# The first six heads' queries by chunks of the model dimension, the general path on one queue, and the row sums counted on VectorE

## The chip, the cores and the metric

The kernel runs on one core of a Trainium2 chip. The metric is device time in microseconds (us), the median of several runs. The engines that matter here are TensorE (PE in the profile; its weight loads are PEld), VectorE (DVE), ScalarE (ACT), GpSimd (POOL) and SyncE (SP), which here only issues transfers and waits. A "q" behind an engine's name (SPq, ACTq) means its instruction sequencer.

## What is computed

Two problems, A and B, of the same shape: queries from an activation `x`, attention over a cache of keys and values with grouped heads (32 query heads, 4 key heads), and an output projection. B = 16 sequences, 32 queries each (512 tokens), model dimension 1024, 512 keys, head size 128, all bfloat16.

```python
q = (x @ wq).reshape(B, Sq, Hq, Dh).transpose(0, 2, 1, 3)
k = jnp.repeat(k_cache, rep, axis=1)          # rep = 8
v = jnp.repeat(v_cache, rep, axis=1)
p = softmax(einsum("bhqd,bhkd->bhqk", q, k) * Dh ** -0.5)
o = einsum("bhqk,bhkd->bhqd", p, v)
out = o.transpose(0, 2, 1, 3).reshape(B, Sq, Hq * Dh) @ wo
# the result is the concatenation of A's and B's out along the last axis
```

## The kernel before

The kernel has two paths. `fast_path` computes everything with a constant shift in the exponential in place of the row's maximum. It keeps the reciprocals of all softmax sums in `rall`, and at the end counts how many of them lie between two limits. If all do, its result stands; if not, `general_path` computes everything anew with the row maximum. With the inputs here the count is full, so the general path is built into the program but not executed: each engine loads the count `ok_i` into a register (L642), compares it and jumps to a short block for the branch not taken (L644), in which the semaphores that the general path would have moved are waited for and brought forward. Then all engines meet at the closing barriers (L671).

The fast path's instructions stand in the order in which they are written (`manual_schedule`), engine by engine.

The beginning: `x` of A (512 tokens by 1024) is loaded in four pieces of 128 whole rows (`load_x`, L469), with the first weights between them. `wq_tiles[0, 0]` and `wq_tiles[0, 1]` hold 4 heads each. `warm_up` runs matmuls on zeros. `transpose_x(tt)` turns one piece of 128 rows into all eight 128-row chunks of `xT` (L507, copies at L510). `first_heads` (L517) computes heads 0 and 1 for the first 256 tokens, and after the other two pieces for the rest. Then `run(units, 52)` issues heads 2 to 7 and 4 matmuls of head 8 from a stream of units. A unit is one matmul of 512 columns: 8 make up a head's queries (`q_units`, L312, copied out by ScalarE at L320), 32 make up a tile of the output projection (`f_units`, L331, copied at L340, stored at L342).

The main loop has 128 slots, one for each pair of a sequence and a key head. A slot issues the loads that a plan gives it, the scores (L368) with their exponential (L376), the values (L432) of four slots before, and 6 or 7 units from the stream in between. Column sums go over VectorE and a small matmul (L387, L396, L404, L413). Loads of K (transposed by the transfer), V, `wq` and `wo` all go through SyncE's queue; stores of the output go through GpSimd's, but for the last two tiles, of 256 columns, which SyncE and ScalarE store.

The end: two passes over `rall` on VectorE (L626) count the flags for each of 32 partitions, 16 units are issued, a matmul with a column of ones adds the partitions (`ok_ps`, L634), VectorE copies the count out (L635), and the remaining units follow. The registers are loaded after all of it.

Of the kernel before, what the change touches and what calls it, by code (L numbers as in the profile page):

```python
# [16 lines left out]
P = 128  # L17
HQ = 32
# [12 lines left out]
def general_path(tc, problems, out_flat):  # L31
# [11 lines left out]
    with ExitStack() as ctx:  # L43
# [10 lines left out]
        for x, k_cache, v_cache, wq, wo, col_off in problems:  # L54
            x_v = x.flatten_outer_dims().rearrange("(t p) d -> p t d", p=P)
            x_sb = wpool.tile([P, TT, D], BF16, name="g_x", tag="g_w")
            nc.sync.dma_start(out=x_sb[:], in_=x_v)
# [10 lines left out]
            for c in range(HQ // WH):  # L68
                wq_sb = wpool.tile([P, DC, WH * DH], BF16, name="g_wq", tag="g_w")
                nc.sync.dma_start(  # L70
                    out=wq_sb[:], in_=wq_v[:, :, c * WH * DH:(c + 1) * WH * DH]
                )
                for hl in range(WH):
                    q_ps = psum.tile([P, NTOK], FP32, name="g_q_ps", tag="g_p", bufs=2)
                    for dc in range(DC):
                        nc.tensor.matmul(
                            q_ps[:],
                            lhsT=wq_sb[:, dc, hl * DH:(hl + 1) * DH],
                            rhs=xT[:, dc, :],
                            start=(dc == 0),  # L80
                            stop=(dc == DC - 1),
                        )
                    nc.scalar.mul(
                        out=qT[:, :, c * WH + hl, :],
                        in_=q_ps[:].rearrange("p (b s) -> p b s", s=SQ),
                        mul=SCALE,
                    )
            oT = big.tile([P, HQ, NTOK], BF16, name="g_oT")
            k_rows = k_cache.rearrange("b g k d -> (b g k) d")
            for b in range(B):  # L90
                kT = kvpool.tile([P, HKV, SK], BF16, name="g_kT")
                r0 = b * HKV * SK
                nc.sync.dma_start_transpose(out=kT[:], in_=k_rows[r0:r0 + HKV * SK, :])
                v_sb = kvpool.tile([P, HKV, KC, DH], BF16, name="g_v")
                nc.sync.dma_start(
                    out=v_sb[:], in_=v_cache[b].rearrange("g (c p) d -> p g c d", p=P)
                )
                for g in range(HKV):
# [53 lines left out]
            for oc in range(NOUT // OCW):  # L152
                wo_sb = wpool.tile([P, HQ, OCW], BF16, name="g_wo", tag="g_w")
                nc.sync.dma_start(out=wo_sb[:], in_=wo_v[:, :, oc * OCW:(oc + 1) * OCW])
                for tt in range(TT):
                    f_ps = psum.tile([P, OCW], FP32, name="g_f_ps", tag="g_p", bufs=2)
                    for h in range(HQ):
                        nc.tensor.matmul(
                            f_ps[:],
                            lhsT=oT[:, h, tt * P:(tt + 1) * P],  # L160
                            rhs=wo_sb[:, h, :],
                            start=(h == 0),
                            stop=(h == HQ - 1),
                        )
                    o_sb = work.tile([P, OCW], BF16, name="g_o_sb")
                    nc.vector.tensor_copy(out=o_sb[:], in_=f_ps[:])
                    c0 = col_off + oc * OCW
                    nc.sync.dma_start(
                        out=out_flat[tt * P:(tt + 1) * P, c0:c0 + OCW], in_=o_sb[:]
                    )  # L170
# [3 lines left out]
def kernel(  # L174
# [35 lines left out]
    def fast_path(ok_i):  # L210
        with ExitStack() as fctx:
# [9 lines left out]
            tc.mark_branch_hint_location(  # L221
                "general",
                "LikelyTaken",
                [nc.sync.engine, nc.scalar.engine, nc.vector.engine, nc.tensor.engine, nc.gpsimd.engine],
            )
# [3 lines left out]
            warm = work.tile([P, NW], BF16, name="warm", tag="p_sb", bufs=6)  # L229
# [10 lines left out]
            one_col = const.tile([P, 1], FP32, name="one_col")  # L240
            nc.vector.memset(one_col[:], 1.0)
            shift = const.tile([P, 1], FP32, name="shift")
            nc.vector.memset(shift[:], SHIFT)
            cnt = const.tile([P, 1], FP32, name="cnt")
            nc.vector.memset(cnt[:], 0.0)
# [35 lines left out]
            def load_k(j):  # L281
                ks = kv_part(j, 1)
                kT = k_tiles[j] = kv.tile([P, GRP, SK], BF16, name="kT")
                if j < NG // GRP:
                    for q in range(GRP):
                        nc.sync.dma_start_transpose(out=kT[:, q, :], in_=ks[q])
# [178 lines left out]
            wq_tiles[0, 0] = blk_tile([P, DC, 4 * DH], "wq_sb")  # L465
            HC = DC // 2

            def load_x(tt):
                nc.sync.dma_start(out=x_sb[:, tt, :], in_=x_v[:, tt, :])  # L469

            def load_first_wq(ns, cs):
                nc.sync.dma_start(out=wq_tiles[0, 0][:, cs, ns], in_=wq_v[:, cs, ns])  # L472

            load_x(0)
            load_x(1)
            load_first_wq(slice(0, 2 * DH), slice(0, HC))
            load_first_wq(slice(0, 2 * DH), slice(HC, DC))
            load_x(2)
            load_x(3)
            load_first_wq(slice(2 * DH, 4 * DH), slice(0, DC))  # L480
            load_wq(0, 1)
            load_k(0)
            load_v(0)
            load_wq(0, 2)
# [3 lines left out]
            warm_ps = psum.tile([P, NW], FP32, name="warm_ps", tag="sums", bufs=1)  # L488

            def warm_up(n):  # L490
                for _ in range(n):
                    nc.tensor.matmul(  # L492
                        warm_ps[:], lhsT=warm[:, 0:P], rhs=warm[:], start=True, stop=True
                    )
# [3 lines left out]
            def transpose_x(tt):  # L498
                ts = slice(tt * P, (tt + 1) * P)
                bank = ("ob", "proj", "sums", "ob")[tt]  # L500
                for cs, where_, copy in (
                    (slice(0, HC), dict(tag="s"), nc.vector.tensor_copy),
                    (slice(HC, DC), dict(tag=bank, bufs=2 if bank == "proj" else 1), nc.scalar.copy),
                ):
                    xT_ps = psum.tile([P, HC, P], BF16, name="xT_ps", **where_)
                    for k, dc in enumerate(range(cs.start, cs.stop)):
                        nc.tensor.transpose(  # L507
                            xT_ps[:, k, :], x_sb[:, tt, dc * P:(dc + 1) * P], ident[:]
                        )
                    copy(out=xT[0][:, cs, ts], in_=xT_ps[:])  # L510

            qT[0, 0] = blk_tile([P, B, REP, SQ], "qT")

            def first_heads(h, t0, t1, dcs):
                ts = slice(t0 * P, t1 * P)
                for dc in dcs:
                    nc.tensor.matmul(  # L517
                        first_q[h][:, ts],
                        lhsT=wq_tiles[0, 0][:, dc, h * DH:(h + 1) * DH],
                        rhs=xT[0][:, dc, ts],  # L520
                        start=(dc == 0),
                        stop=(dc == DC - 1),
                    )

            lower, upper = range(HC), range(HC, DC)
            warm_up(5)
            transpose_x(0)
            transpose_x(1)
            first_q = [psum.tile([P, NW], FP32, name="q_ps", tag="proj") for _ in range(2)]
            warm_up(2)  # L530
            for dcs in (lower, upper):
                for h in range(2):
                    first_heads(h, 0, 2, dcs)
            transpose_x(2)
            transpose_x(3)
            for h in range(2):
                for tt in (2, 3):
                    first_heads(h, tt, tt + 1, range(DC))
            for h, copy in enumerate((nc.vector.tensor_copy, nc.scalar.copy)):
                copy(  # L540
                    out=qT[0, 0][:, :, h, :],
                    in_=first_q[h][:].rearrange("p (b s) -> p b s", s=SQ),
                )

            def stream():
                for h in range(2, HQ):
# [6 lines left out]
                for tts in ((0, 1), (2,)):  # L553
                    for nh in range(NH):
                        for tt in tts:
                            yield from f_units(1, tt, nh * NW, NW, nc.gpsimd)
# [5 lines left out]
            run(units, (REP - 2) * DC + 4)  # L562
# [59 lines left out]
            sq = blk_tile([QD, NG * 2 * REP], "sq", FP32)  # L622
            cnt2 = const.tile([P, 2], FP32, name="cnt2")
            nc.vector.memset(cnt2[:], 0.0)
            for k, (lim, op) in enumerate(((1.0 / SUM_HI, ALU.is_ge), (1.0 / SUM_LO, ALU.is_le))):
                nc.vector.tensor_scalar(  # L626
                    out=sq[:], in0=rall[0:QD].rearrange("p j n -> p (j n)"),
                    scalar1=lim, scalar2=0.0, op0=op, op1=ALU.add,
                    accum_out=cnt2[0:QD, k:k + 1],
                )  # L630
            nc.vector.tensor_tensor(out=cnt[:], in0=cnt2[:, 0:1], in1=cnt2[:, 1:2], op=ALU.add)
            run(units, 16)
            ok_ps = psum.tile([1, 1], FP32, name="ok_ps", tag="s")
            nc.tensor.matmul(ok_ps[:], lhsT=cnt[:], rhs=one_col[:], start=True, stop=True)  # L634
            nc.vector.tensor_copy(out=ok_i[:], in_=ok_ps[:])  # L635
            run(units, 1 << 20)

    flag = ctx.enter_context(tc.tile_pool(name="flag", bufs=1))
    ok_i = flag.tile([1, 1], I32, name="ok_i")
    fast_path(ok_i)  # L640
    total = 2 * 2 * NG * QW
    ok = nc.values_load(ok_i[0:1, 0:1], min_val=0, max_val=total,  # L642
                        skip_runtime_bounds_check_because="only compared")
# [32 lines left out]
```

## Time and profile before

| | |
|---|---|
| median of 6 runs | 348.68 us (347.97 to 348.80) |
| profiled execution | 348.74 us |
| its span, first to last instruction | 346.8 us |
| TensorE busy | 338.7 us, 2145 matmuls |
| VectorE, ScalarE busy | 265.8 and 189.2 us |
| bytes moved by transfers | 71.70 MB, 207 GB/s over the span |
| `L331` (output projection), 512-column matmuls | 127.6 us busy |
| `L312` (queries), 512-column matmuls | 124.1 us busy |
| last matmul ends | 342.46 us |

The span is shorter than the time of its execution by what lies before the first and behind the last instruction. Matmuls overlap in the pipeline, so the profile's mean duration of one (366 ns at L331) is longer than the distance between two starts; that distance is read from a row of many matmuls. A row of the timeline has the start, the time from the first instruction's start to the last one's end, the engine, the line, the operation, the tile written and the tiles read, the shape and the number of instructions; in brackets how long the engine had been idle before and what ended that. A row of one line's instructions has the engine, the operation and its number, the shortest, median and longest duration in ns, and the start of the first and the last.

### The profile page before, as it was taken

The numbers are of one execution on the slowest core, as the hardware profiler recorded it, in microseconds if no ns is written. First come the engines' busy times: TensorE is split into PE (matmuls) and PEld (weight loads), VectorE is DVE, ScalarE is ACT, GpSimd is POOL, SyncE is SP. The second block draws the span as 40 slices with busy tenths as digits, with TensorE's granted clock in tenths as the row PEclk, the third lists the DMA queues.
The fourth block names the chain that finished last, engine by engine and source line by source line (L and its number), as shares of the span: only waits on it lengthen the run. The fifth ranks groups of instructions, "written<-read, shape, count | busy, mean of one in ns | idle before, by whom it ended". The sixth has DMA issues, their size and how long they took to land.

```text
span 346.8 us, 5422 instructions
## 1 busy us (share of the span) xinstructions
PE 338.7 (98%) x2145; PEld 218.2 (63%) x2185; DVE 265.8 (77%) x340; ACT 189.2 (55%) x213; POOL 8.9 (3%) x21
## 2 busy tenths in 40 slices
PE   8999999999999999999999999999999999999994
PEld 5556666666666666666666666666666666666554
DVE  2117888888888888888888888888988888888610
ACT  2447666666666766666655445555455545555000
POOL 0000000000000000000000000000000000000010
PEclk9999999999999999999999999999999999999999
DMA  7999999999998999999999449995669984400000
GB/s 227 240 306 339 166 256 263 263 262 260 274 203 191 217 243 237 291 271 272 271 307 205 109 127 289 350 255 122 137 188 290 295 210 115 114 33 2 15 33 19
DMA packets 125068, 71.70 MB, mean 207 GB/s; under 512 B 73616, under 2 KB 124048, under 8 KB 125040
## 3 DMA queue, kind: packets, MB, share of 16 engines
q1 hardware_dynamic: 124176, 69.29, 81.4%
q0 software_dynamic: 720, 1.97, 1.6%
q8 instruction: 18, 0.29, 0.4%
q14 instruction: 10, 0.08, 0.1%
q10 hardware_dynamic: 144, 0.07, 0.1%
HBM read 51.38 MB, written 2.10 MB: 154 GB/s over the span
## 4 chain that ended last, share of the span: by engine, by line
PE 96%; DMA 2%; issue 1%; SPq 1%; ACT 0%; ACTq 0%
PE f_ps L331 31%; PE q_ps L312 30%; PE ob L432 17%; PE s_ps L368 17%; DMA x_sb<-in_A_x_dram 2%; PE q_ps L517 1%; SPq L469 0%; SPq L472 0%; PE xT_ps L507 0%; PE sums L404 0%; ACT o_sb L340 0%; PE ok_ps L634 0%; SPq L671 0%; ACTq L340 0%
## 5 line engine op out<-in xcount | busy, mean ns | idle before, releaser
L376 ACT ACTIVATE p_sb<-s_ps,shift 128x1024 bf16<-128x1024 f32 x128 | 142.7, 1115 | 101.6 <-PE s_ps L368 69.4
L387 DVE TRANSPOSE_TENSOR_REDUCE parts<-p_sb 128x32 f32<-128x1024 bf16 x128 | 158.9, 1241 | 45.6 <-ACT p_sb L376 45.5
L331 PE MATMUL f_ps<-wo_sb,oT 128*128 128x512 bf16 (+1 forms) x524 | 127.6, 366 | 0.5
L312 PE MATMUL q_ps<-xT,wq_sb 128*128 128x512 bf16 x476 | 124.1, 379 | 0.5
L432 PE MATMUL ob<-p_sb,v_sb 128*128 128x256 bf16 x512 | 76.8, 273 | 0.7
L368 PE MATMUL s_ps<-qT,kT 128*128 128x256 bf16 x512 | 76.8, 273 | 0.5
L331 PEld LDWEIGHTS <-oT 128*128 128x128 bf16 x544 | 53.0, 98 | 34.8
L368 PEld LDWEIGHTS <-kT 128*128 128x128 bf16 x512 | 56.9, 113 | 24.7
L312 PEld LDWEIGHTS <-wq_sb 128*128 128x128 bf16 x496 | 48.5, 98 | 35.8 <-DMA wq_sb<-in_A_wq_dram 0.2
L432 PEld LDWEIGHTS <-v_sb 128*128 128x128 bf16 x512 | 50.1, 98 | 19.9
L454 DVE TENSOR_TENSOR oT<-r,ob 128x512 bf16<-128x512 f32 x64 | 44.0, 687 | 8.8 <-PE ob L432 2.3
L320 ACT CAST qT<-q_ps 128x512 bf16<-128x512 f32 x62 | 36.2, 584 | 21.1 <-PE q_ps L312 19.0
L418 DVE STREAM_TRANSPOSE r<-rall 128x512 f32<-128x512 f32 x64 | 44.2, 691 | 1.1
L340 ACT CAST o_sb<-f_ps 128x512 bf16<-128x512 f32 (+1 forms) x17 | 9.5, 559 | 23.2 <-PE f_ps L331 14.6
L342 POOL DMA_DIRECT2D out_dram<-o_sb x15 | 8.2, 550 | 327.3 <-ACT o_sb L340 327.3
L396 DVE TENSOR_REDUCE cs<-parts 128x32 fp32r<-128x128 f32 x32 | 12.0, 375 | 1.1
L404 PE MATMUL sums<-cs,fold 128*128 128x32 f32 x32 | 11.7, 367 | 0.0
L413 DVE RECIPROCAL rall<-sums 128x32 f32<-128x32 f32 x32 | 10.2, 320 | 0.5 <-PE sums L404 0.5
L404 PEld LDWEIGHTS sums<-cs,fold 128*128 128x128 f32 x32 | 6.1, 190 | 3.8
L510 DVE COPY xT<-xT_ps 128x512 bf16<-128x512 bf16 x4 | 1.7, 424 | 5.5 <-PE xT_ps L507 5.5
L510 ACT COPY xT<-xT_ps 128x512 bf16<-128x512 bf16 x4 | 2.3, 586 | 5.6 <-PE xT_ps L507 5.5
L492 PE MATMUL warm_ps<-warm 128*128 128x512 bf16 x7 | 3.2, 597 | 1.3 <-DVE warm L230 1.3
(26 smaller groups left out, 21.9 us busy)
## 6 DMA issues: line engine op xcount, KB each, us to landing
v_sb<-in_A_v_cache_dram SPq DMA_DIRECT2D x16, 512.0 KB, 4.3
wq_sb<-in_B_wq_dram SPq DMA_DIRECT2D x8, 1024.0 KB, 6.2
wo_sb<-in_A_wo_dram SPq DMA_DIRECT2D x8, 1024.0 KB, 6.7
v_sb<-in_B_v_cache_dram SPq DMA_DIRECT2D x16, 512.0 KB, 4.3
wo_sb<-in_B_wo_dram SPq DMA_DIRECT2D x8, 1024.0 KB, 8.9
wq_sb<-in_A_wq_dram SPq DMA_DIRECT2D x7, 1024.0 KB, 7.3
out_dram<-o_sb POOLq DMA_DIRECT2D x15, 128.0 KB, 2.1
x_sb<-in_A_x_dram SPq DMA_DIRECT2D x4, 256.0 KB, 4.1
```

The lines of the kernel that those rows point to most:

```text
L312: nc.tensor.matmul(ps[:], lhsT=w[:, dc, (h % 4) * DH:(h % 4 + 1) * DH], rhs=xT[pr][:, dc, :], start=(dc == 0), stop=(dc == DC - 1),)
L320: nc.scalar.copy(out=qT[pr, g][:, :, hl, :], in_=ps[:].rearrange("p (b s) -> p b s", s=SQ),)
L331: nc.tensor.matmul(ps[:, 0:width], lhsT=oT[pr, tt][:, h, :], rhs=wo_tiles[pr, nh, h // REP][:, h % REP, off:off + width], start=(h == 0), ...
L368: nc.tensor.matmul(s_ps[:, c, :], lhsT=kT[:, i % GRP, c, :], rhs=qT[pr, g][:, b, :, :].rearrange("p h s -> p (h s)"), start=True, stop=True,)
L376: nc.scalar.activation(out=p_sb[:], in_=s_ps[:], func=ACTF.Exp, bias=shift[:], scale=SCALE)
L387: nc.vector.tensor_reduce(out=parts[k][:, q, :, :].rearrange("p c h -> p (c h)"), in_=st[i]["p"][:].rearrange("p c (h s) -> p (c h) s", s=SQ),
L396: nc.vector.tensor_reduce(out=cs[:], in_=parts.pop(k)[:].rearrange("p q c h -> p q h c"), axis=AX.X, op=ALU.add,)
L404: nc.tensor.matmul(sums[:], lhsT=fold[:].rearrange("p r s -> p (r s)"), rhs=cs[:].rearrange("p q h -> p (q h)"), start=True, stop=True,)
L413: nc.vector.reciprocal(out=rall[:, k, :], in_=quad.pop(k)[:])
L418: nc.vector.transpose(out=r[:].rearrange("p n s -> p (n s)"), in_=rall[:, k, o * 2 * REP:(o + 1) * 2 * REP] .unsqueeze(2).to_broadcast([P, ...
L432: nc.tensor.matmul(ob[j][:, q, :], lhsT=v_sb[:, i % GRP, c, :], rhs=st[i]["p"][:, c, :], start=(c == 0), stop=(c == KC - 1),)
L454: nc.vector.tensor_tensor(out=out, in0=rcp.pop(j)[:].rearrange("p (q h) s -> p q h s", h=REP), in1=ob.pop(j)[:].rearrange("p q (h s) -> p ...
```

## The change

- The beginning goes by chunks of the model dimension. `x` is loaded in four column pairs of two 128-column chunks each (the first pair in two halves of 256 tokens), in runs of 512 bytes. The weights of heads 0 to 7 lie in two tiles `w0`, each with four 128-row chunks of all eight heads, loaded after the piece of `x` that they meet. `transpose_x(k)` transposes chunks 2k and 2k+1 for all tokens. Six PSUM accumulators, heads 0 to 5, take one chunk after the other; the transposes of the next pair stand in the middle of every second chunk. Heads 6 and 7 follow with all eight chunks each. The copies are shared between VectorE and ScalarE. The warm-ups are 128 columns wide: 19 before the transposes, 2 and 4 between them.
- The order of the first loads: one quarter of the first K block, then `wq` for heads 8 to 11, then the rest of K, and V. Before: two blocks of `wq` with all of the first K and V between them.
- 5 units of head 8 are issued before the main loop; it was 4.
- The stores of B's first two token tiles go through SyncE's queue instead of GpSimd's.
- The count: the flags' sums are added by a 32x32 block transpose and a reduction on VectorE; the matmul is gone. The registers are loaded 40 units after it, in the middle of TensorE's last stretch, and not at the end.
- In the general path every transfer is issued by GpSimd; K is loaded as it lies and transposed on TensorE.
- The mark for the branch hint stands near the end of the fast path in the text.

```diff
 # general_path, at each of its transfers
-            nc.sync.dma_start(out=x_sb[:], in_=x_v)
+            nc.gpsimd.dma_start(out=x_sb[:], in_=x_v)
...
-                nc.sync.dma_start_transpose(out=kT[:], in_=k_rows[r0:r0 + HKV * SK, :])
+                for g in range(HKV):
+                    kT_ps = psum.tile([P, KC, P], BF16, name="g_kT_ps", tag="g_t", bufs=2)
+                    for kc in range(KC):
+                        nc.tensor.transpose(kT_ps[:, kc, :], k_sb[:, g, kc, :], ident[:])
...
 # fast_path, the beginning
-            load_x(0)
-            load_x(1)
-            load_first_wq(slice(0, 2 * DH), slice(0, HC))
-            load_first_wq(slice(0, 2 * DH), slice(HC, DC))
-            load_x(2)
-            load_x(3)
-            load_first_wq(slice(2 * DH, 4 * DH), slice(0, DC))
-            load_wq(0, 1)
-            load_k(0)
-            load_v(0)
-            load_wq(0, 2)
+            w0 = [blk_tile([P, HC, REP * DH], "w0_sb") for _ in range(2)]
+            def load_x(k, ts=slice(0, TT)):
+                cs = slice(2 * k * P, (2 * k + 2) * P)
+                nc.sync.dma_start(out=x_sb[:, ts, cs], in_=x_v[:, ts, cs])
+            load_x(0, slice(0, TT // 2))
+            load_x(0, slice(TT // 2, TT))
+            load_w0(slice(0, 1), slice(0, HALF * DH))
+            load_w0(slice(0, 1), slice(HALF * DH, REP * DH))
+            load_w0(slice(1, 2))
+            for k in range(1, DC // 2):
+                load_x(k)
+                load_w0(slice(2 * k, 2 * k + 2))
+            load_k(0, slice(0, 1))
+            load_wq(0, 2)
+            load_k(0, slice(1, GRP))
+            load_v(0)
             load_k(1)
             load_v(1)
...
-            warm_up(5)
-            transpose_x(0)
-            transpose_x(1)
-            ...
+            warm_up(19)
+            transpose_x(0, (2, 4))
+            ...
+            for dc in range(DC - 2):
+                for h in range(NF):
+                    if dc % 2 and h == NF // 2:
+                        transpose_x(dc // 2 + 1)
+                    first_head(first_q[h], h, dc)
+            for h in (0, 2, 4, 1, 3, 5):
+                for dc in (DC - 2, DC - 1):
+                    first_head(first_q[h], h, dc)
+                evacuate(first_q[h], h)
+            for h, tag in zip(range(NF, REP), ("ob", "sums")):
+                q_ps = psum.tile([P, NW], FP32, name="q_ps", tag=tag, bufs=1)
+                for dc in range(DC):
+                    first_head(q_ps[:], h, dc)
+                evacuate(q_ps[:], h)
...
-                for tts in ((0, 1), (2,)):
+                for tts, eng in (((0, 1), nc.sync), ((2,), nc.gpsimd)):
...
-            run(units, (REP - 2) * DC + 4)
+            run(units, 5)
 # the end
-            nc.vector.tensor_tensor(out=cnt[:], in0=cnt2[:, 0:1], in1=cnt2[:, 1:2], op=ALU.add)
-            run(units, 16)
-            ok_ps = psum.tile([1, 1], FP32, name="ok_ps", tag="s")
-            nc.tensor.matmul(ok_ps[:], lhsT=cnt[:], rhs=one_col[:], start=True, stop=True)
-            nc.vector.tensor_copy(out=ok_i[:], in_=ok_ps[:])
-            run(units, 1 << 20)
+            nc.vector.transpose(out=tally_t, in_=tally)
+            nc.vector.tensor_reduce(out=cnt, in_=tally_t[0:1], axis=AX.X, op=ALU.add)
+            nc.vector.tensor_copy(out=ok_i[:], in_=cnt)
+            run(units, 40)
+            tc.mark_branch_hint_location(...)
+            ok = nc.values_load(ok_i[0:1, 0:1], min_val=0, max_val=total, ...)
+            run(units, 1 << 20)
+            return ok
```

## Prediction

> **What bounds the kernel now.** I first read the page's busy shares and its chain of waits, to see which engine sets the end.
>
> ```profile
> PE 338.7 (98%) x2145; PEld 218.2 (63%) x2185; DVE 265.8 (77%) x340; ACT 189.2 (55%) x213; POOL 8.9 (3%) x21
> ...
> PE 96%; DMA 2%; issue 1%; SPq 1%; ACT 0%; ACTq 0%
> ```
>
> Columns of the first: busy time, share, instructions; the second is the chain's shares. TensorE carries 96% of it; only the stretch before its steady stream and the one after its last matmul are left. So I read the timeline of the first 12 us next.
>
> ```profile
> 1.29 2.31 PE L492 MATMUL warm_ps<-warm 128*128 128x512 bf16 x5 [1.29 <-DVE warm L230]
> ...
> 3.63 1.89 PE L507 MATMUL xT_ps<-ident,x_sb 128*128 128x128 bf16 x16
> ...
> 4.28 0.42 DVE L510 COPY xT<-xT_ps 128x512 bf16<-128x512 bf16 x1 [1.82 <-PE xT_ps L507]
> ...
> 5.31 0.84 PE L492 MATMUL warm_ps<-warm 128*128 128x512 bf16 x2
> ...
> 5.99 1.91 PE L517 MATMUL q_ps<-xT,wq_sb 128*128 128x256 bf16 x16
> ...
> 8.14 1.29 PE L507 MATMUL xT_ps<-ident,x_sb 128*128 128x128 bf16 x16 [0.24 <-DMA x_sb<-in_A_x_dram]
> ...
> 9.27 2.11 PE L517 MATMUL q_ps<-xT,wq_sb 128*128 128x128 bf16 x32
> ...
> 11.27 2.97 PE L312 MATMUL q_ps<-xT,wq_sb 128*128 128x512 bf16 x12
> ...
> 13.64 8.80 PE L312 MATMUL q_ps<-xT,wq_sb 128*128 128x512 bf16 x40
> ```
>
> Two of A's heads are done at 11.27. From there matmuls follow each other without a hole: the row of 40 in 8.80 us, less a duration of 0.38 and divided by 39, gives 0.216 us per 512 columns. The five warm-ups are 0.43 apart, so the array ran at half speed; the x16 row at 5.99 has 0.109 per 256 columns, full speed. The granted clock's records put the turn at 5.79. Until 11.27 TensorE did 2 heads (16 x 0.216 = 3.5 us) and 32 transposes (1.8 us): 5.3 us of work, so about 6 us are start, slow clock and waiting.
>
> Then the end. The last matmul ends at 342.46, and the timeline shows the last copy and store.
>
> ```profile
> 342.53 0.37 ACT L340 CAST o_sb<-f_ps 128x256 bf16<-128x256 f32 x1 [3.12 <-PE f_ps L331]
> 342.93 0.38 ACTq L342 DMA_DIRECT2D out_dram<-o_sb  x1
> ```
>
> The instructions of L644 and of L671, asked for by line (duration in ns, first and last start), show what follows.
>
> ```profile
> L644 SPq EVENT_SEMAPHORE  x8: 17/17/17, 344.6 to 345.1; - x8
> ...
> L671 SPq EVENT_SEMAPHORE  x14: 17/28/28, 345.2 to 346.8; - x14
> ...
> L671 SPq DRAIN  x3: 7/7/13, 345.9 to 346.3; - x3
> ```
>
> The store lands at 344.59. Only then does SyncE walk 8 semaphores of the branch not taken (L644, 344.60 to 345.20), then 12 of the 14 at L671 (345.20 to 345.95), and then the closing barriers up to 346.83. The first wait of the 8 is that store's.
>
> **The end (saves 1.28).** In the built program the general path now issues on GpSimd's queue alone, so SyncE's share of the branch not taken is one jump, and GpSimd has five waits there instead. The 12 waits at L671 stay, but the ScalarE store now holds the eighth hardware semaphore, which is the last of the 12. So eleven are walked before the store lands. After it there remain that last wait and the barriers: 345.88 to 346.83, 0.95 us from the landing instead of 346.83 - 344.60 = 2.23. That is 1.28 us. Bounds: 0.6 (only the 8 go) to 1.35. GpSimd's waits lie at 337 to 338 (its last store lands at 338.4), and its jump over 264 unexecuted instructions has over 6 us of cover. ScalarE loses its 0.48 us register load after the last store; it had been under the store's flight.
>
> **The count (saves 0.2).** The ok_ps matmul goes: from the f_ps matmul before it to the one behind took 0.44 us instead of 0.216. On VectorE a 32x64 transpose, a reduction and a copy replace it; the nearest rows, 0.69 (128x512 transpose), 0.38 (L396) and 0.15 (L635), end the count by 331.6. TensorE's register load (0.49 us before, at 340.3) now stands 56 half-width matmuls before the end: 342.46 - 56 x 0.109 = 336.3, less the 2.1 us its sequencer ran ahead: 334.2, so the count has 2.6 us of cover. That same lead covers the 0.49 us, since the array has matmuls queued; I take 0, bound 0.5.
>
> **The beginning (saves about 1.0).** Heads 0 to 5 now start once the first two 128-row chunks of x's columns are transposed, so TensorE no longer waits for whole rows of x. The steps:
> 1. Start. The first two x pieces are 256 KB together, as much as the old first load, which released the transposes at 3.63; in 512 B runs I give them 3.7 for both. Before, VectorE's copy started 0.65 after the first transpose and ended at 4.70. Here half the transposes run earlier (3.2), two warm-ups and four more follow, so the copy ends near 4.78 and head matmuls begin at 4.85. Bounds 4.6 to 5.5.
> 2. Work. 64 matmuls x 0.216 = 13.82, and 24 transposes x 0.056 = 1.34 (the eight at 8.14 are 0.056 apart).
> 3. Slow clock. If the turn comes at 5.79 again, 0.94 us run at half speed: 0.47 lost.
> 4. Landings. Per pair of chunks 786 KB must land: at the rates of the table by windows (last column below: 243 GB/s from 4 to 5 us, 345 from 9 to 11), 2.3 to 3.2 us, against 12 x 0.216 + 0.45 = 3.04 us of TensorE. Before, 1.5 MB were in at 8.77, and chunks 2 and 3 (1.57 MB so far) are needed at 8.5: I take 0.2 of waiting. The last weights, 3.1 MB in all, landed at 13.53 before and are needed at 14.7.
>
> ```profile
> 4.00:5.00 1.00, 1.00 (x13) 1.00 (x11) 0.42 (x1) 0.30 (x1) 0.00 (x0) 1.00 0.85 243
> ...
> 9.00:11.00 2.00, 2.00 (x37) 1.88 (x35) 0.90 (x2) 0.97 (x2) 0.00 (x0) 1.00 1.10 345
> ...
> 13.50:17.00 3.50, 3.50 (x18) 1.60 (x17) 0.00 (x0) 1.22 (x3) 0.00 (x0) 1.00 1.50 174
> 17.00:21.50 4.50, 4.50 (x23) 1.96 (x20) 0.00 (x0) 1.41 (x3) 0.00 (x0) 1.00 1.12 337
> ```
>
> Sum: 4.85 + 13.82 + 1.34 + 0.47 + 0.2 = 20.68 for eight heads, against 11.27 + 48 x 0.216 = 21.64: 0.96 saved. Bounds -0.3 (start 5.5, 0.8 of waits) to 1.5.
>
> What is late next? wq for heads 8 to 11 landed at 21.51 before and was waited for (0.2 us). It moves ahead of three K transposes and V, so 1.2 MB follow the 3.1 MB: from 13.5 at 337 GB/s it is in at 17.0, at 174 GB/s at 20.3; both before 20.68. The next wq landed at 28.62; the same SyncE issues stand ahead of it, and it is needed at 29.5 (30.50 before, less 0.96): 0.9 of cover, then a loss one for one. The fifth unit, the copies of eight heads (four at 0.69 on VectorE, which is idle there) and the smaller warm tile cost nothing: head 7's copy ends at 21.6 and scores begin at 21.8.
>
> A rule against this is in the Trainium skill, "TensorE: Matmul & The Clock Gate", Part 4: transposes do not count as activity for the clock. The trace had 16 of them from 3.63 to 5.52 and full speed by 5.99, which speaks for counting them. By the rule the turn could come one window (3.4 us on that page) later, which by step 3 would cost an estimated 1.7 us.
>
> **The queues.** Four of B's stores move from GpSimd to SyncE, between K and V loads, and SyncE waits there for ScalarE's copies. The load behind each is needed at least 7 slots later (7 x 2.34 = 16 us) and takes 4.3 to 6.7 us to land. Nothing. In both built programs the branch hint is the first instruction of every engine, so moving its mark does nothing. The general path's new code is not executed.
>
> **Sum.** 0.96 + 0.22 + 1.28 = 2.46. The profiled execution took 348.74 (span 346.83, 1.91 outside it), 0.06 over the median of 348.68. 348.74 - 2.46 = 346.3, span 344.4.
>
> **Rivals.**
> - Landings set the pace of the beginning. Were the queue to hold 243 GB/s throughout, 3.15 MB from 2.0 us take to 15.0, plus 0.5 of receipt; 12 + 16 matmuls follow (6.05): 21.6. The beginning saves nothing: 347.2. For it: x is now in 512 B runs. Against: 304 to 345 GB/s from 7 to 11 us with wq's 512 B runs in it. 17%.
> - Another wait takes the place of SyncE's: GpSimd or an instruction fetch ends after the store lands, and the 1.28 stays: 347.6. Against: GpSimd was through at 339. 9%.
> - Slower: the clock. From 4.85 on, every microsecond at half speed costs 0.5, where before the wait for x (until 8.09) hid it. The point that decides is 5.79 + 2 x 2.46 = 10.7: a later turn makes the kernel slower, by over 0.2% from 12.1. The turn came 4.5 us after the first warm-up (1.29 to 5.79). Were that stretch to begin anew with the head matmuls, after the small gaps between warm-ups and transposes, the turn would be at 9.35 and cost 1.8 more: 348.1. Were it to begin anew once more at the wait for chunks 2 and 3 (8.5), the turn at 13.0 would cost 3.6 more: 349.9. For it: gaps and transposes now lie between the early matmuls. Against: the turn at 5.79 with as many transposes and a gap at 3.6. 9%, of which 6% slower.
> - The forecast 62%, stalls at the later wq 3%.
>
> **How the numbers follow.** A measurement of this kernel can tell about 0.2% (0.7 us) from no change. Faster takes the forecast (62), most of the first two rivals (14 of 17, 7 of 9) and the stalls (3): 0.86. Same takes the rest of those (3 + 2) and the clock's first case (3): 0.08. Slower is the clock's second case: 0.06. The forecast alone spans 345.4 (start 4.6, full rates, tail 1.35) to 346.9; up to 347.7 takes in the first two rivals.
>
> **What would show it.** Right: head matmuls of 512 columns from 4.85 with 0.43 then 0.216 between starts, the stream's first (head 8) at 20.7, no L644 row of SyncE, 0.95 us from the last landing to the end. Wrong: the stream's first matmul after 21.6, holes on w0_sb, matmuls 0.43 apart after 6 us, a wait of TensorE at its register load, or over 2 us behind the last store.

## The result, and the profile after

The changed kernel takes 347.42 us (346.86 to 350.05) where the kernel before takes 348.67: a ratio of 0.9969 [0.9961, 0.9977]. The gain is 1.25 us between the medians and 1.1 us by the ratio, into which the longest runs enter more. The forecast was 346.3, a gain of 2.4. The direction holds, but about half of the gain is missing: 347.42 lies beyond what the forecast alone spanned (345.4 to 346.9), and inside the range only because that took in two rivals (up to 347.7). The profiled execution of the changed kernel took 347.07 us, span 345.26.

TensorE bounds it as before. The page's busy shares and the chain's shares:

```profile
PE 338.5 (98%) x2128; PEld 218.0 (63%) x2169; DVE 268.1 (78%) x342; ACT 186.9 (54%) x210; POOL 6.8 (2%) x17
...
PE 92%; SPq 3%; DMA 3%; issue 1%; DVE 0%; ACT 0%; ACTq 0%
```

The chain now has 3% of SyncE and 3% of transfers in it, where it had 1% and 2%. So there is a place at which TensorE follows a load. The timeline of TensorE from 4 to 24 us shows it (start, length, line, tiles, count, in brackets the idle time before and what ended it):

```profile
4.91 3.21 PE L526 MATMUL q_ps<-xT,w_sb 128*128 128x512 bf16 x9
7.96 0.61 PE L513 MATMUL xT_ps<-ident,x_sb 128*128 128x128 bf16 x8
8.62 0.59 PE L526 MATMUL q_ps<-xT,w_sb 128*128 128x512 bf16 x2
9.38 2.12 PE L526 MATMUL q_ps<-xT,w_sb 128*128 128x512 bf16 x9 [0.16 <-DMA w_sb<-in_A_wq_dram]
...
14.82 6.93 PE L526 MATMUL q_ps<-xT,w_sb 128*128 128x512 bf16 x30
21.59 1.24 PE L313 MATMUL q_ps<-xT,wq_sb 128*128 128x512 bf16 x5
```

Head matmuls start at 4.91, as forecast. At 9.38 the third chunk starts, and a load released it. Head 8, the stream's first, starts at 21.59, where the forecast had 20.7 and the kernel before 21.63. The beginning gave nothing. The chain of waits between 0 and 14 us names the transfer, issued at 3.81 and 5.53 us on its way:

```profile
3.81 5.53 DMA w_sb<-in_A_wq_dram
9.34 0.05 issue
```

From the first exponential (0.18 later than before, which is one more unit of head 8 ahead of it) to the last, nothing moves against before. At the end, the last copy and store in the timeline, and the closing semaphores of L698 (duration in ns, first and last start):

```profile
342.26 0.37 ACT L341 CAST o_sb<-f_ps 128x256 bf16<-128x256 f32 x1 [3.12 <-PE f_ps L332]
342.66 0.38 ACTq L343 DMA_DIRECT2D out_dram<-o_sb  x1
```

```profile
L698 SPq EVENT_SEMAPHORE  x14: 17/28/877, 340.4 to 345.2; - x14
...
L698 SPq DRAIN  x3: 7/7/13, 344.4 to 344.7; - x3
```

The store lands at 344.29. SyncE had begun its walk at 340.4 and had eleven of twelve waits behind it; 0.97 us are left, where there were 2.24.

### The profile page after: what moved, and what is told of

Same layout as the page of the kernel before. It is cut to its first block, busy times and chain, and to the rows that moved or that the text cites. A ratio compares the mean times of both kernels' runs of the same rounds, so it can differ in the third digit from the quotient of the medians.

```text
span 345.3 us, 5389 instructions
## 1 busy us (share of the span) xinstructions
PE 338.5 (98%) x2128; PEld 218.0 (63%) x2169; DVE 268.1 (78%) x342; ACT 186.9 (54%) x210; POOL 6.8 (2%) x17
## 4 chain that ended last, share of the span: by engine, by line
PE 92%; SPq 3%; DMA 3%; issue 1%; DVE 0%; ACT 0%; ACTq 0%
PE f_ps L332 31%; PE q_ps L313 25%; PE s_ps L369 16%; PE ob L433 16%; PE q_ps L526 3%; SPq L287 2%; DMA w_sb<-in_A_wq_dram 2%; DMA v_sb<-in_A_v_cache_dram 1%; SPq L471 0%; SPq L474 0%; PE xT_ps L513 0%; DVE qT L536 0%; SPq L257 0%; PE sums L405 0%; SPq L295 0%
## 5 line engine op out<-in xcount | busy, mean ns | idle before, releaser
L313 PE MATMUL q_ps<-xT,wq_sb 128*128 128x512 bf16 x429 | 113.6, 379 | 0.4
L313 PEld LDWEIGHTS <-wq_sb 128*128 128x128 bf16 x448 | 43.8, 98 | 30.4
L321 ACT CAST qT<-q_ps 128x512 bf16<-128x512 f32 x56 | 32.6, 582 | 13.9 <-PE q_ps L313 11.8
L526 PE MATMUL q_ps<-xT,w_sb 128*128 128x512 bf16 x62 | 15.5, 400 | 0.4 <-DMA w_sb<-in_A_wq_dram 0.2
L343 POOL DMA_DIRECT2D out_dram<-o_sb x11 | 6.1, 553 | 329.2 <-ACT o_sb L341 329.2
L526 PEld LDWEIGHTS <-w_sb 128*128 128x128 bf16 x64 | 6.3, 102 | 8.0 <-issue 1.5
```

The source lines that it names most:

```text
L313: nc.tensor.matmul(ps[:], lhsT=w[:, dc, (h % 4) * DH:(h % 4 + 1) * DH], rhs=xT[pr][:, dc, :], start=(dc == 0), stop=(dc == DC - 1),)
L321: nc.scalar.copy(out=qT[pr, g][:, :, hl, :], in_=ps[:].rearrange("p (b s) -> p b s", s=SQ),)
L526: nc.tensor.matmul(q_ps, lhsT=w0[dc // HC][:, dc % HC, h * DH:(h + 1) * DH], rhs=xT[0][:, dc, :], start=(dc == 0), stop=(dc == DC - 1),)
```

## Experiments

All ratios are to the kernel before, run beside the variant on the same chip. Times inside a run are from its one profiled execution.

**e1: the old beginning, everything else changed.** The diff takes `load_x`, the first weights, `transpose_x` and `first_heads` back to the form before.

> The beginning of before (x in rows, heads 0 and 1 first), all the rest as after the change. Theory 1 (the new beginning saves nothing, the whole gain is the end and the count): time as after the change, 347.4, last matmul at 342.2 to 342.3, about 1.0 us from the last store's landing to the end. Rival (the new beginning does save about 1 us and something later gives it back, the moved stores for one): 348.4 or a last matmul past 343 here, or 346.5 if what gave it back goes with it.

347.41 us, 0.9963 [0.9950, 0.9977]: the same as the changed kernel, although its last store sits on another semaphore and it takes 1.15 us from the last landing to the end (0.18 more). Scores start at 22.63 here and at 22.67 in the changed kernel. So the new beginning is worth nothing; a loss of 0.2, which the 0.18 would make of it, is smaller than the intervals.

**e2: the old general path**, its transfers on SyncE and K transposed by the transfer.

```diff
-                nc.gpsimd.dma_start(...)   # at each transfer of general_path
+                nc.sync.dma_start(...)
```

> The general path as before (its transfers on SyncE's queue, K transposed by the transfer), all the rest as after the change. Theory (the gain at the end is SyncE's walk over the semaphores of the branch not taken): 8 waits of SyncE return behind the last store, last landing to end grows from 0.95 to about 2.2 us, time 348.7. Rival (the gain at the end comes from loading the registers earlier): 347.4, span 345.3.

348.42 us, 0.9995 [0.9986, 1.0004]. The gain is gone, but not all of it by the end: from the last landing to the end it takes 1.70 us, 0.73 more than in the changed kernel. The semaphores of the branch not taken are back in SyncE's walk, here L663:

```profile
L663 SPq EVENT_SEMAPHORE  x8: 17/17/17, 340.8 to 345.0; - x8
```

Seven of the eight were walked before the store landed at 344.97, since the store holds the eighth; only the twelve closing waits (0.73) came behind it. So the 1.28 are 0.73 for the general path's queue and about 0.55 for the semaphore on which the last store happens to be. The split depends on the order: with the queue moved first and the store still on the first semaphore, seven closing waits of 0.06 each (measured below) would stay behind it, an estimated 0.85 for the queue and 0.43 for the semaphore. The rest of the loss in e2's profiled execution is a late landing at the beginning (below).

**e3 and e4: the weights of chunks 2 to 7 in single chunks; e4 also loads the weights of heads 12 to 15 ahead of the second K block.**

```diff
-                load_w0(slice(2 * k, 2 * k + 2))
+                load_w0(slice(2 * k, 2 * k + 1))
+                load_w0(slice(2 * k + 1, 2 * k + 2))
 # e4 alone
+            load_wq(0, 3)
             load_k(1)
```

> The weights of chunks 2 to 7 in one transfer for each chunk, not one for each pair; all else as after the change. Theory 1 (the landing of the weights of chunks 2 and 3 together, at 9.34, holds the beginning): the first matmul of chunk 2 moves from 9.38 to between 8.4 and 9.1 and head 8 from 21.6 to between 20.9 and 21.3; but three more issues of 0.45 on SyncE put the weights of heads 12 to 15, which landed at 30.50 and were needed at 30.68, near 32, so a hole of some 1 us opens there, and the time is 347.3 to 347.9. Rival (the late turn of the clock, 7.20 against 5.79, holds the beginning): chunk 2 starts where chunk 1 ends, no hole at 9, head 8 moves by under 0.3, 347.4.

> As the run with one transfer for each chunk, and the weights of heads 12 to 15 issued ahead of the second K block. Theory 1 with the late weights as the next wait: no hole at the fifth slot, head 8 at 20.9 to 21.3, last matmul 341.5 to 341.9, 346.8 to 347.1. Rival (the clock): 347.3 to 347.5.

e3: 347.57, 0.9974 [0.9962, 0.9986]. Chunk 2's weights landed at 9.39 all the same, and those of heads 12 to 15 at 31.00, later than needed: 0.3 of a hole. e4: 347.20, 0.9964 [0.9951, 0.9976]; chunk 2 at 8.61, heads 12 to 15 at 25.12, no hole, head 8 at 20.86. Up to chunk 7 the two have the same loads, so 9.39 and 8.61 show how far it varies from one execution to the next. With the split, e3, e4, e9 and e12 had chunk 2 at 8.61 to 9.39, 8.9 in the mean; unsplit, six profiled runs had 9.34 to 10.03, 9.7 in the mean. Both lose 0.31 at the end (1.28 instead of 0.97): three more hardware transfers shift the last store by three semaphores, to one with five waits behind it.

**e9: e4 with that put right**, three of B's four stores back on GpSimd's queue.

```diff
-                for tts, eng in (((0, 1), nc.sync), ((2,), nc.gpsimd)):
+                for tts in ((0, 1), (2,)):
...
+                            eng = nc.sync if (tt, nh) == (0, 0) else nc.gpsimd
```

> The kernel of e4 (one transfer for each weight chunk, weights of heads 12 to 15 ahead of the second K block), with three of B's four SyncE stores put back on GpSimd's queue, so that ScalarE's last store again holds the eighth hardware semaphore. Theory (each wait that stands behind the last store in SyncE's walk costs 0.06 us): 0.97 us from the last landing to the end in place of e4's 1.28, nothing else moves, head 8's first matmul between 20.8 and 21.2; median 346.9, 0.31 below e4's. Rival (the semaphore is not what sets it, it varies from run to run): 1.28 again, 347.2. Rival (stores on GpSimd's queue cost a wait): holes of TensorE at the output projection of B's first two token tiles, above 347.4.

346.54 us, 0.9945 [0.9931, 0.9959], the lowest median here: 0.97 from the last landing to the end, head 8 at 20.88. The profiled executions of e4 and e9 are 0.34 apart (346.70 and 346.36), as the 0.31 at the end asks; the medians are 0.66 apart, with intervals that overlap. The start of chunk 2 and of head 8 in e9's timeline:

```profile
8.20 2.59 PE L528 MATMUL q_ps<-xT,w_sb 128*128 128x512 bf16 x11
...
20.88 1.24 PE L313 MATMUL q_ps<-xT,wq_sb 128*128 128x512 bf16 x5
```

**e8: all four stores back on GpSimd.**

> The changed kernel with the four stores of B's first two token tiles back on GpSimd's queue. Four hardware transfers less: ScalarE's last store gets the fourth hardware semaphore, so that four more waits stand behind it. Theory (the store on SyncE's queue is worth nothing by itself, each wait 0.06): nothing moves before the last landing, 1.21 instead of 0.97 us from there to the end, 347.66. Rival (the semaphore does not matter): 347.42. Rival (GpSimd's waits at the branch come later than the last landing with four more stores before them): above 347.9.

347.84, 0.9978 [0.9969, 0.9987]: 1.22 us at the end. With e1 and e10 (1.15, three waits behind the store), e15 (1.09, two), e3 and e4 (1.28, five) the end is 0.97 + 0.06 for each wait behind the store's.

**e10: without the transfers of chunks 2 to 7.**

```diff
             for k in range(1, DC // 2):
                 load_x(k)
-                load_w0(slice(2 * k, 2 * k + 2))
...
-                    lhsT=w0[dc // HC][:, dc % HC, h * DH:(h + 1) * DH],
+                    lhsT=w0[0][:, dc % 2, h * DH:(h + 1) * DH],
```

> The changed kernel without the transfers of the weight chunks 2 to 7 of the first eight heads (1.5 MB): the matmuls of those chunks read chunks 0 and 1 again, so heads 0 to 7 are computed from wrong weights. Work and order of the instructions stay. ScalarE's last store gets the fifth semaphore here, three more waits behind it: 0.18 us more at the end. Theory (the landing of the weights of chunks 2 and 3 takes the beginning's gain): no hole at chunk 2; head 8's first matmul at start 4.9 + 13.82 + 1.34 + half of the time from 4.9 to the clock's turn: 20.6 for a turn at 5.8, 21.2 for one at 7.2, where the changed kernel had 21.59; the whole 0.2 to 0.8 below the changed kernel (346.7 to 347.2 with the 0.18). Rival (the clock alone takes it, and the turn stays at 7.2): 21.5 or more, 347.4 to 347.6.

346.97, 0.9951 [0.9937, 0.9964]. No hole at chunk 2; head 8 at 21.07 with a turn of the clock at 6.21. The sum by work and clock (start, work and half of the time up to the turn, as in the expectation) gives 20.67; the other 0.4 is x, whose second piece landed at 7.73, with the transposes at 7.77. So without these weights 0.5 of the 0.96 comes back, and x is the next landing in the way.

**e6 and e12: the changed kernel, and e9, with one warm-up instead of 25.**

```diff
-            warm_up(19)
-            transpose_x(0, (2, 4))
+            warm_up(1)
+            transpose_x(0)
```

> The changed kernel with one warm-up matmul instead of 25: TensorE idles until x lands, so the clock's turn comes later. The forecast's step 3 prices each microsecond at half speed at 0.5 from 4.85 on; with the landing of chunk 2 at 9.34 the first 0.3 us of that are covered. Theory (the turn follows about 4.5 us behind the first steady work, which is now the transposes at 3.1): turn at 7.6 to 7.9, at most 0.1 us lost, 347.4 to 347.5. Rival (the transposes do not count, the turn follows 4.5 us behind the first head matmul at 4.85): turn at 9.35, 0.8 us lost, 348.2. Rival (the wait for chunk 2 starts it anew): turn at about 13.5, head 8 at 24.4, 350.

> The kernel of e9 with one warm-up matmul instead of 25. In e6 two things came on top of the clock: the late weights of heads 12 to 15 (0.7 us of holes) and a long flight of the last store. Here those weights come early. Theory (only the clock is left: a turn 1 to 3 us later than with warm-ups, less what the landings cover): turn at 7.6 to 9.4, head 8's first matmul 0.4 to 1.2 later than e9's 20.88, median 346.9 to 347.8. Rival (e6's 1.66 us are all the clock's): 348.2.

e6: 349.08, 1.0009 [1.0000, 1.0019]. e12: 348.47, 0.9992 [0.9982, 1.0001]. Both lose far more than the clock's share. The turn came at 8.10 and 7.46, and in the profiled executions head 8 was 0.39 and 0.52 later than with warm-ups. But that is again the landing of chunk 2 (9.73 and 9.14, plus the 12.25 that is worked out below); by work and clock head 8 would have come at 21.52 and 21.18. So e12's expectation got its 0.4 to 1.2 by luck. In e6 late weights of heads 12 to 15 (31.71) took 0.7. The largest part is at the other end of the kernel: the last store was 3.4 and 3.6 us from issue to landing instead of 1.6. The view of the DMA queues over four microseconds there, first e6, then the changed kernel (packets, MB, share of the 16 engines):

```profile
q10 hardware_dynamic: 144, 0.07, 6.0%
q8 instruction: 1, 0.02, 2.0%
q14 instruction: 1, 0.01, 0.8%
...
out_dram<-o_sb ACTq DMA_DIRECT2D x1, 64.0 KB, 3.4
```

```profile
q10 hardware_dynamic: 144, 0.07, 5.5%
q14 instruction: 1, 0.01, 0.5%
...
out_dram<-o_sb ACTq DMA_DIRECT2D x1, 64.0 KB, 1.6
```

In e6 a 16 KB packet of queue q8, instructions, started at 344.94 and took 1.28 us; fifteen engines had finished the store by 345.35, the sixteenth at 347.20. In e12 likewise (344.06 for 1.01; 344.06 and 346.05). Packets do not name their engine in these traces, but the store's remaining packets start at 346.19 and 345.05, just as the instruction packet ends (346.22 and 345.07). The changed kernel's packet of that queue lies at 341.33, between two stores. Dropping 24 warm-ups at the start seems to have moved that fetch into the last store's flight; that the shorter program is why was not tried apart. This is read from one execution of each: e6's took 349.97, 0.9 above its median, and e12's other runs lie between 347.63 and 348.91.

**e7: the old count and register loads.**

> The changed kernel with the count as it was before: a matmul with a column of ones adds the partitions, and the registers are loaded after TensorE's last matmul. The last store keeps its semaphore. Theory (the forecast's step on the count): one gap of 0.44 instead of 0.22 between matmuls near 339, last matmul and last landing 0.22 later, 347.64. ScalarE's register load lies under the store's flight: nothing. Rival (moving the register loads ahead of the last 56 matmuls is worth something by itself, since an engine's load stands behind the last store): more than 0.5 above the changed kernel, 347.9. Rival (the count was hidden): 347.42.

347.70, 0.9969 [0.9959, 0.9980]: 0.28 above the changed kernel's median, though the ratio is the same, so the times alone do not show 0.2. The trace does: from the last exponential to the last matmul it takes 0.23 longer (23.43 for 23.20), as the 0.22 of the forecast.

**e5: the weights of heads 12 to 15 early, alone.**

> The changed kernel with the weights of heads 12 to 15 loaded ahead of the second K block, nothing else. Theory (in the changed kernel they land at 30.50, 0.2 before they are needed, and cost nothing as long as the beginning is not faster): they land near 25, median 347.42 or at most 0.2 less. Rival (in many runs they are late, as in e6's 31.7, and this is part of what took the gain): 347.0 or less.

347.33, 0.9963 [0.9950, 0.9976]: they land at 25.16 and the time hardly moves. In the changed kernel they are just in time.

**e11 and e13: e9 with a second queue for the first loads.** e11 issues the weights of chunks 0 and 1 on ScalarE, e13 half of x's first piece and half of chunk 0. In both, ScalarE's table load now stands behind its issues.

```diff
 # e11
-            load_w0(slice(1, 2))
+            load_w0(slice(1, 2), eng=nc.scalar)   # and both halves of chunk 0
 # e13
-            load_x(0, slice(TT // 2, TT))
+            load_x(0, slice(TT // 2, TT), nc.scalar)   # and chunk 0's second half
```

> The kernel of e9 with the weights of chunks 0 and 1 (three transfers) issued on ScalarE's queue, ahead of its table load, so that SyncE issues x and the weights of chunks 2 to 7 some 1.4 us earlier. Theory (the early landings are late because one queue issues 128 KB every 0.5 us): the weights of chunk 1 land about 1 us earlier than e9's 6.72, those of chunk 2 by 7.9 instead of 8.63, the 0.55 hole at chunk 1 goes, head 8's first matmul at 4.7 + 15.16 + half of the time from 4.7 to the clock's turn: 20.0 to 21.1; median 346.0 to 346.5. Rival (the 16 DMA engines are the limit between 4.5 and 7.5, not the issues): the same landings, 346.5. Rival (ScalarE's first copy comes later behind its issues and its table load): head matmuls from 5.2 or later, 346.8.

> The kernel of e9 with the second half of x's first piece and the second half of chunk 0's weights issued on ScalarE's queue (two transfers), so that x stays ahead of all weights and SyncE issues everything from chunk 1's weights on 1.0 us earlier. Theory (the pace of the first issues sets the early landings, as far as x is not held back): both x pieces land by 3.3, head matmuls from 4.3 to 4.6, weights of chunk 1 by 6.3 instead of 6.72, of chunk 2 by 8.2, median 346.1 to 346.4. Rival (the transfer engines are the limit whatever the order of issue): chunk 1 at 6.7 again, 346.5. Rival (x is held back by the second queue as in e11): x at 4.0 or later, 347 or more.

e11: 348.17, 0.9987 [0.9979, 0.9996]; e13: 346.77, 0.9946 [0.9931, 0.9960], no better than e9 (its profiled execution, with a turn at 10.08, took 348.46 and is its longest run). Chunk 1's weights landed at 6.84 and 6.57 (6.72 in e9), though issued 1 us earlier. The Trainium skill, "DMA: Bandwidth & Descriptors", "Rules for kernel authors", says that several issuing queues bring no bandwidth since all use the same 16 engines, and only save issue time; these landings agree. In e11 x lost what the weights took. The timeline of TensorE in e11:

```profile
4.05 0.61 PE L515 MATMUL xT_ps<-ident,x_sb 128*128 128x128 bf16 x4 [0.76 <-DMA x_sb<-in_A_x_dram]
...
5.40 0.61 PE L515 MATMUL xT_ps<-ident,x_sb 128*128 128x128 bf16 x4 [0.53 <-DMA x_sb<-in_A_x_dram]
...
6.31 3.61 PE L528 MATMUL q_ps<-xT,w_sb 128*128 128x512 bf16 x9
```

TensorE waits twice for x, head matmuls start at 6.31, and the clock turns only at 9.39.

**e14: x in runs of 2 KB. e15: x's first piece and chunk 0's weights in one transfer each, two issues fewer.**

```diff
 # e14: x_sb laid out by pieces, each read as whole rows
+            x_sb = blk_tile([P, DC // 2, TT, 2 * P], "x_sb")
 # e15
-            load_x(0, slice(0, TT // 2))
-            load_x(0, slice(TT // 2, TT))
+            load_x(0)
```

> The changed kernel with x loaded in runs of 2 KB (1 KB for the two halves of the first piece) instead of 512 bytes: x_sb is laid out piece by piece, and each transfer reads whole rows of x, so the tokens and columns are mixed up and the queries of heads 0 to 7 are wrong; order, bytes and instructions stay. Theory (512-byte runs slow the first 1.57 MB): the weights of chunks 2 and 3 land by 8.8 instead of 9.3 to 10.0, head 8's first matmul at 21.0 to 21.2, 346.9. Rival (the pace of issue, or one late engine of the 16): 9.3 to 10.0 again, 347.4.

> The changed kernel with the first piece of x in one transfer and the weights of chunk 0 in one: two issues less, so that SyncE issues everything behind them 1.0 us earlier. Two hardware transfers less also move ScalarE's last store to the sixth hardware semaphore, two more waits, 0.12 us at the end. Theory (the pace of the first issues delays the first 1.57 MB): the weights of chunks 2 and 3 land by 8.8, head matmuls start 0.1 to 0.3 later than 4.9, head 8's first matmul at 21.1 to 21.4, 347.1 to 347.3. Rival (the transfer engines are the limit): landing 9.3 to 10.0 again, 347.5 to 347.7.

e14: 347.09, 0.9957 [0.9942, 0.9971]; chunk 2's weights at 9.52, inside the 9.34 to 10.03 of the runs with 512 bytes, head 8 at 21.78: the runs of 512 bytes are not it. e15: 347.37, 0.9971 [0.9954, 0.9988]; the weights, issued 0.95 earlier, landed at 8.93, 0.4 to 1.1 earlier than in the changed kernel's order, but head matmuls began at 5.30 and the clock turned at 7.58: 21.64 again.

## Why the prediction was right at the end and wrong at the beginning

**The end** (1.28) was right: 2.24 became 0.97. What it did not separate is that about half a microsecond of it (0.43 to 0.55, by e2) rests on the number of hardware transfers in the whole kernel, which decides the last store's semaphore (e2, e8, e4 against e9). Its rival, another wait in SyncE's place, did not come: GpSimd was through its waits at 340.0, two microseconds later than the forecast's 337 to 338, but still 4 before the last landing. The instruction fetch that this rival named does occur, in another form: in e6 and e12 it goes with a late last store.

**The count** (0.22) was right, by e7's trace. VectorE was done at 331.18 (the forecast had 331.6), and TensorE's register load at 332.9, 0.49 long, left no hole.

**The beginning** (0.96) was wrong, and the term that failed is its step 4, the landings: 0.2 of waiting. Chunks 2 and 3 were needed at 8.5 by the forecast and landed at 9.34: 0.84 in its own terms. In the profile the later turn of the clock filled most of that time with slower matmuls, so only 0.16 of it shows as a hole. Start (4.91 for 4.85) and work were right. Two sums, of which the later decides, give head 8's first matmul within 0.05 in every run of the table: the landing of the transfer that holds chunk 2's weights plus 12.25 (from 9.34 to 21.59 in the changed kernel: 52 matmuls, 16 transposes and 0.1), or the run's start + the forecast's work of 15.16 + half of the time from the start to the clock's turn. (e3, e6 and e7, which are not in the table, follow the landing too: 9.39, 9.73 and 9.58 give 21.64, 21.98 and 21.83, and 21.65, 21.98 and 21.84 were measured.)

| run | start | turn | chunk 2 landed | landing + 12.25 | by work and clock | measured |
|---|---|---|---|---|---|---|
| changed | 4.91 | 7.20 | 9.34 | 21.59 | 21.22 | 21.59 |
| e2 | 4.92 | 7.24 | 10.03 | 22.28 | 21.24 | 22.28 |
| e5 | 4.77 | 5.08 | 9.75 | 22.00 | 20.09 | 22.00 |
| e8 | 4.79 | 4.54 | 9.83 | 22.08 | 19.95 | 22.08 |
| e14 | 4.69 | 4.86 | 9.52 | 21.77 | 19.94 | 21.78 |
| e12 | 4.57 | 7.46 | 9.14 | 21.39 | 21.18 | 21.40 |
| e9 | 4.66 | 4.90 | 8.63 | 20.88 | 19.94 | 20.88 |
| e4 | 4.92 | 6.34 | 8.61 | 20.86 | 20.79 | 20.86 |
| e15 | 5.30 | 7.58 | 8.93 | 21.18 | 21.60 | 21.64 |
| e11 | 6.31 | 9.39 | 8.20 | 20.45 | 23.01 | 23.05 |
| e13 | 5.58 | 10.08 | 8.58 | 20.83 | 22.99 | 23.01 |

In e8 the clock turned before the first head matmul, and head 8 is still 0.5 later than in the changed kernel. Its timeline:

```profile
4.79 1.46 PE L526 MATMUL q_ps<-xT,w_sb 128*128 128x512 bf16 x6
6.95 0.82 PE L526 MATMUL q_ps<-xT,w_sb 128*128 128x512 bf16 x3 [0.70 <-DMA w_sb<-in_A_wq_dram]
...
9.88 2.12 PE L526 MATMUL q_ps<-xT,w_sb 128*128 128x512 bf16 x9 [0.90 <-DMA w_sb<-in_A_wq_dram]
```

Full speed only makes the wait longer. So the landings set the pace, the rival given 17%. It had the right mechanism, but its 21.6 is luck: it let the last weights land at 15.5, at 243 GB/s throughout, and these landed at 13.94 and held nothing; the landing with chunk 2 did. The table by windows, first before, then changed, has the share of the DMA engines and GB/s in its last two columns. (The granted clock ahead of them reads 1.00 because there is no record before the turn; up to 7.0 us the matmuls of the changed kernel start 0.43 apart, half speed.)

```profile
2.00:4.00 2.00, 1.97 (x8) 0.67 (x7) 0.40 (x5) 0.11 (x1) 0.00 (x0) 1.00 0.90 280
...
5.00:7.00 2.00, 2.00 (x17) 1.41 (x16) 0.42 (x1) 0.88 (x2) 0.00 (x0) 1.00 1.03 321
```

```profile
2.00:4.00 2.00, 1.93 (x20) 1.66 (x18) 0.38 (x3) 0.10 (x1) 0.00 (x0) 1.00 0.74 227
4.00:5.00 1.00, 1.00 (x11) 0.96 (x10) 0.42 (x1) 0.36 (x1) 0.00 (x0) 1.00 0.62 214
5.00:7.00 2.00, 2.00 (x7) 0.60 (x6) 0.00 (x0) 0.23 (x1) 0.00 (x0) 1.00 0.95 258
7.00:9.00 2.00, 1.95 (x15) 1.08 (x14) 0.42 (x1) 0.39 (x1) 0.00 (x0) 1.00 0.98 335
```

The forecast took the rates of the old order of loads for a new one. Up to 7 us the changed one moved 1.18 MB (227 x 2 + 214 + 258 x 2) where the old one moved 1.45; at 335 GB/s the difference is 0.78 us, of the size of the 0.57 by which the same 1.5 MB were later (9.34 for 8.77). Nor is a landing a rate: the first of the 16 engines had its part of chunks 2 and 3 at 8.03, the last at 9.34. Why is settled in part only. The runs of x are not it (e14), and no packet of the instruction queues starts in the changed kernel's first 15 us. A wait for half the bytes helps (8.9 for 9.7 in the mean, e3 and e4). Fewer issues ahead seem to help (e15: 8.93, one execution), a second queue by itself does not. Which engine is late, and why it is in each run, stays open.

Six profiled runs with the same loads (the changed kernel, e2, e5 to e8) had chunk 2 between 9.34 and 10.03, the changed kernel's own profile being the earliest. So the median run may lose a little in the beginning: 1.27 + 0.22 - 1.25 leaves 0.24 lost, by the ratio 0.4; e1 says 0.2. The intervals are too wide to tell these from nothing.

**The clock** (step 3) turned at 7.20, not 5.79, which by that step costs 0.7 more; the landing covered it. With the landing in time, head 8 would still have come at 21.22 in this execution instead of 20.7, so step 3 was a second weak term: it took the one turn that had been seen. As a rival on the slow side the clock needs a turn after 10.7, which did not occur in the changed kernel; in e11 and e13, where TensorE waited for x ahead of the first transposes, it came at 9.39 and 10.08, close to that.

**The next weights** (heads 12 to 15) were said to land at 28.62 again. They landed at 30.50 and were needed at 30.68. The claim that the same issues stand ahead of them overlooked the three more transfers of the beginning: the first K transpose is issued at 6.88 instead of 5.42, and the weights at 23.80 instead of 22.01. A beginning as fast as forecast would have stalled there, as e3 did.

## To carry to other kernels

When a stage's loads are reordered, sum the stage twice, once as the landing of the last engine's part plus all work behind it and once as the start plus all work, and take the later; rates read from the old order of loads do not carry over. Every issue added at the head of a queue can delay all that follow (here the weights of heads 12 to 15 were issued 1.8 us later), so the issue time of the next loads belongs in the sum too. At the end of a kernel, list what is walked after the last store lands: here each semaphore wait behind the store's own cost 0.06 us, and the number of transfers in the whole kernel decided how many there were.

## What the runs showed of the hardware that was not expected

- The clock's turn varies from execution to execution: in one execution each of ten kernels with the same 25 warm-ups and no hole before the first transposes it came between 4.54 and 7.24 us. The Trainium skill, "TensorE: Matmul & The Clock Gate", Part 1, gives a free-running window of about 3.4 us and a turn that varies by 0.5 us either way; here it is 1.35 either way. With a hole of 0.46 to 0.76 us between warm-ups and transposes (e15, e13, e11) it came at 7.58, 10.08 and 9.39.
- With a 16 KB instruction packet of 1.0 to 1.3 us in flight together with the last store, one engine's part of that store landed 1.9 to 2.0 us after the other fifteen (e6, e12).
- Between 4.5 and 7.5 us single 2 KB packets took up to 0.67 us in the changed kernel (0.66 before, up to 1.35 in e3), with a median of 0.084 in each.
